# Softmax sums from a column of ones, keys laid by group, and two pieces of expert work moved into step 11 of a fused window-attention and expert kernel

## The chip, the cores and the metric

The kernel runs on one core of one Trainium2 chip. The metric is the device time of one execution in microseconds (us). Before the change three runs took 647.63, 648.9 and 649.51 us, a median of 648.9. One further execution was profiled: it took 648.28 us, of which 646.4 us are the span from the first to the last instruction. Engines are named as the profile names them: PE is TensorE (matmuls; PEld its weight loads), DVE is VectorE, ACT is ScalarE, POOL is GpSimd, and SP is the engine whose queue issues most of the DMAs.

## What is computed

Two layers follow one another: causal attention in a window of 64 positions, and a layer of eight experts of which each token uses one.

```python
# q, k, v: (8, 8, 576, 64) float32: batch, heads, positions, head size
scores = q @ k^T / 8                       # only 0 <= pos_q - pos_k < 64 counts, the rest is masked
attn   = exp(scores - max) / (sum + 1e-9)
x      = (attn @ v), heads side by side    # 4608 tokens x 512
logits = x @ w_gate + modality_bias[modality_id]       # 4608 x 8
e      = argmax(logits);  gate = softmax(logits)[e]
out    = gate * (relu(x @ w1[e]) @ w2[e])              # w1 512 x 1024, w2 1024 x 512, float32
```

## The kernel before

**Tiling.** The 4608 tokens are 72 blocks of 64 positions, and two blocks are a *pair* (36 pairs of 128 rows). A window of 64 means that a block needs its own keys and those of the block before it. Two pairs are a *group* (4 blocks); queries and keys are loaded and turned (transposed on PE) by group.

**Steps.** The attention is written as a loop over `s` (40 steps), software pipelined by hand: step `s` makes the scores of pair `s` (`scores`, PE), masks them and takes each row's minimum of the negated scores (`minima`, DVE, eight heads, L577), takes the exponentials (`exps`, ACT, eight heads, L589, each with a row sum by `accum_out`), turns the exponentials of pair `s-1` (`probs_t`, PE, copied out by ACT at L598), multiplies those of pair `s-2` with the values (`values`, PE, L615), divides by the sum (`values_out`, DVE: a reciprocal at L621 and one product of 128x512 at L623), turns the result (`x_t`) and makes the gate's logits of pair `s-3`. In each step two *heads* pieces of the next group follow: in even steps the keys, `K0` (heads 0 to 3) and `K1` (heads 4 to 7), in odd steps the queries, `Q0` and `Q1`. Each is four transposes on PE and one copy of 128x512 out of PSUM (`heads_out`, L539); K1 is copied by ACT, the other three by DVE. Between these parts `tick(n)` emits up to n small operations on DVE from a list: the routing of tokens, and tables of a few words that choose experts and rows.

The order is fixed by the program (a manual schedule): every engine runs its list in that order, and semaphores order the engines against each other. [...]

**Values.** `vo` holds a pair's own values. `ve` holds for the first of the two blocks the rows in the order in which its window stands: its lower half is copied by POOL from the pair's own rows, its upper half by DVE from the pair before (`swap_v`, L495).

**Expert work.** From step `FIRST` = 12 on, four *pieces* of expert work are put into the gaps of each step (`gap`, `slot_pieces`). A slot is 256 tokens of one expert: `x_part` 0 and 1 turn its rows (L254) and split them into a high and a low part on ACT and DVE (L192, L193), eight `first` pieces multiply by w1 (L279, 12 matmuls of 128x256), eight `second` pieces by w2 (L301, 6 matmuls of 128x512). The rows of a slot come from scratch memory by a DMA that `fetch` issues (L203), behind the indirect DMAs by which POOL scattered them there (L716). The weights of two experts are loaded and split piece by piece from step 3 on (`weights`, L111 on ACT and L116 on DVE). When the attention is over, the remaining pieces follow one another alone.

**PSUM banks.** There are eight: two `tp`, two for scores, one `av`, and `em`, `y0`, `y1` that belong to the expert work. `turn_bank(s)` lends the last three to the attention as long as `s < FIRST - 1`, so up to step 10.

**Start.** Group 0 is turned in two halves by `first_pair(0)` and `first_pair(1)`, one before the scores of step 0 and one between them and the minima. ACT's queue first issues four query DMAs and then the DMAs of the modality numbers, the bias and the gate weights.

## Time and profile before

| | profiled execution |
|---|---|
| its time / its span | 648.28 us / 646.4 us |
| PE busy | 620.0 us (96% of the span) |
| PEld busy | 554.6 us (86%) |
| DVE busy | 367.7 us (57%) |
| ACT busy | 299.4 us (46%) |
| POOL busy | 137.4 us (21%) |
| DMA | 88.07 MB, mean 136 GB/s |
| HBM read, written | 67.49 MB, 23.91 MB |

The page gives shares of the whole span, and the program has stages. From 100 us on, PE is busy for 19.25 to 20.00 us of each stretch of 20 up to 640 us; from 20 to 100 us it is busy for 16.5 to 17.5 of each 20. In the timeline of PE the scores of step 0 start at 9.45 us, those of step 1 at 15.37, of step 2 at 22.25, of step 5 at 40.41, of step 11 at 76.43, of step 12 at 84.85 and of step 13 at 97.65 us. A row of the timeline has start, duration, engine, line, operation, what is written and read, the count, and in brackets the idle time of the engine before it with what ended it. A row of windows has for one stretch the busy time of every engine, the granted clock of PE, and the DMA's share and rate.

### The profile page before, as it was taken

What the parts mean: (1) busy time and instruction counts of PE and PEld (TensorE: products, weight loads), DVE (VectorE), ACT (ScalarE), POOL (GpSimd) and SP (SyncE); (2) the same over time, 40 slices, a digit from 0 to 9 for tenths busy, and PEclk for the clock granted to TensorE, in tenths of its full rate; (3) what the DMA queues carried; (4) which work ended last, traced back from release to release, by engine and by line L of the source; (5) the groups of instructions that cost most, each with busy time, mean ns of one, the idle gap of its engine ahead of it and who ended that gap; (6) DMA issues with size and microseconds to landing.
All of it is one profiled execution on the core that took longest, in us unless ns stands there. A gap on an engine that the chain in (4) does not pass through costs nothing.

```text
span 646.4 us, 17286 instructions
## 1 busy us (share of the span) xinstructions
PE 620.0 (96%) x6508; PEld 554.6 (86%) x6509; DVE 367.7 (57%) x1494; ACT 299.4 (46%) x932; POOL 137.4 (21%) x314
## 2 busy tenths in 40 slices
PE   6888889999999999999999999999999999999996
PEld 4677779898989888889998898899898999989986
DVE  2889967777767686766655365122214524757611
ACT  2789875756565646555544111111113513555411
POOL 4315330232142212320322220011011101101102
PEclk9999989999999999999999999999999999999999
DMA  9988975764876754553412124421041732677300
GB/s 164 195 186 216 212 197 132 196 161 120 181 171 153 159 144 103 144 133 82 132 51 83 50 99 171 157 67 66 23 173 45 236 113 85 218 247 227 120 1 36
DMA packets 138885, 88.07 MB, mean 136 GB/s; under 512 B 116746, under 2 KB 116784, under 8 KB 138672
## 3 DMA queue, kind: packets, MB, share of 16 engines
q1 hardware_dynamic: 130112, 67.44, 42.2%
q0 software_dynamic: 5856, 18.92, 7.8%
q10 hardware_dynamic: 2832, 0.59, 0.6%
q8 instruction: 52, 0.85, 0.6%
q14 instruction: 33, 0.27, 0.2%
HBM read 67.49 MB, written 23.91 MB: 141 GB/s over the span
## 4 chain that ended last, share of the span: by engine, by line
PE 50%; DVE 0%; ACT 0%; issue 0%; POOL 0%; POOLq 0%; ACTq 0%
PE y L301 22%; PE em L279 12%; PE sp L279 10%; PE tp L439 1%; PE y L352 1%; PE av L615 1%; PE em L254 1%; PE tp L254 1%; PE sp L327 0%; PE em L327 0%; PE tp L640 0%; PE sp L563 0%; DVE xa L623 0%; ACT ss L589 0%; DVE hl L288 0%
## 5 line engine op out<-in xcount | busy, mean ns | idle before, releaser
L301 PE MATMUL y<-Whi,hh 128*128 128x512 f32 x288 | 118.7, 412 | 0.0
L301 PE MATMUL y<-Wlo,hh 128*128 128x512 f32 x288 | 112.9, 392 | 0.0
L301 PE MATMUL y<-Whi,hl 128*128 128x512 f32 x288 | 112.8, 392 | 0.0
L589 ACT ACTIVATE ss<-ss,mn 128x128 f32<-128x128 f32 x288 | 112.5, 397 | 0.0
L279 PE MATMUL em<-xh,Whi 128*128 128x256 f32 x400 | 103.5, 293 | 1.2 <-ACT xh L192 0.7
L279 PE MATMUL em<-xh,Wlo 128*128 128x256 f32 x400 | 98.5, 280 | 0.0
L288 DVE SCALAR_TENSOR_TENSOR hl<-em,hh 128x512 fp32r<-128x512 f32 x50 | 34.5, 690 | 92.9 <-ACT hh L287 91.3
L312 POOL DMA_INDIRECT out_dram<-y,id x36 | 37.3, 1036 | 224.6 <-DVE y L309 145.9
L279 PEld LDWEIGHTS em<-xh,Whi 128*128 128x128 f32 x400 | 75.9, 190 | 2.6 <-ACT xh L192 0.9
L279 PEld LDWEIGHTS em<-xh,Wlo 128*128 128x128 f32 x400 | 75.8, 190 | 0.9
L287 ACT ACTIVATE hh<-em 128x512 fp32r<-128x512 f32 x50 | 29.6, 592 | 93.3 <-PE em L279 89.4
L577 DVE CUSTOM_DVE_ANT_0 ss<-sp,masks 128x128 f32<-128x128 f32 x288 | 63.5, 286 | 13.4 <-PE sp L563 13.4
L598 ACT COPY pT<-tp 128x512 f32<-128x512 f32 x58 | 32.2, 589 | 78.0 <-PE tp L439 78.0
L301 PEld LDWEIGHTS y<-Whi,hl 128*128 128x128 f32 x288 | 54.1, 188 | 12.3
L279 PE MATMUL em<-xl,Whi 128*128 128x256 f32 x400 | 63.4, 281 | 0.0
L301 PEld LDWEIGHTS y<-Whi,hh 128*128 128x128 f32 x288 | 54.1, 188 | 7.5
L301 PEld LDWEIGHTS y<-Wlo,hh 128*128 128x128 f32 x288 | 54.3, 188 | 7.1
L589 ACT ACTIVATION_READ_ACCUMULATOR ss<-ss,mn 128x1 f32 x288 | 55.8, 194 | 0.0
L716 POOL DMA_INDIRECT xs_scratch<-xa,idx x36 | 36.3, 1007 | 89.1 <-DVE lm L659 26.9
L279 PEld LDWEIGHTS em<-xl,Whi 128*128 128x128 f32 x400 | 54.2, 189 | 0.0
L288 DVE SCALAR_TENSOR_TENSOR hl<-sp,hh 128x512 fp32r<-128x512 f32 x22 | 15.2, 692 | 61.1 <-ACT hh L287 61.1
L615 PEld LDWEIGHTS av<-ve,pT 128*64 128x64 f32 x576 | 36.4, 138 | 15.2 <-issue 7.4
(242 smaller groups left out, 1243.6 us busy)
## 6 DMA issues: line engine op xcount, KB each, us to landing
xt<-xs_scratch SPq DMA_DIRECT2D x18, 514.0 KB, 4.0
vo<-in_v_dram SPq DMA_DIRECT2D x32, 256.0 KB, 4.1
y<-in_moe_w_dram SPq DMA_DIRECT2D x32, 256.0 KB, 4.0
vo<-in_moe_w_dram SPq DMA_DIRECT2D x24, 256.0 KB, 3.5
ss<-in_moe_w_dram SPq DMA_DIRECT2D x24, 256.0 KB, 3.8
qk<-in_k_dram SPq DMA_DIRECT2D x18, 256.0 KB, 5.5
qk<-in_q_dram SPq DMA_DIRECT2D x18, 256.0 KB, 4.9
xs_scratch<-xs_scratch SPq DMA_DIRECT2D x8, 514.0 KB, 6.0
```

The lines of the kernel that those rows point to most:

```text
L254: nc.tensor.transpose(out=tp[:, n * P:(n + 1) * P].bitcast(F32R), in_=xt[:, t, c * P:(c + 1) * P].bitcast(F32R), identity=ident_r)
L279: nc.tensor.matmul(out=hb[:, i * TP:(i + 1) * TP], lhsT=w[buf][:, c0:c0 + P], rhs=x[:, c * TP:(c + 1) * TP], start=(n == 0), stop=(n == le ...
L287: nc.scalar.activation(out=hh, in_=hb, func=AF.Relu),
L288: nc.vector.scalar_tensor_tensor(out=hl, in0=hb, scalar=0.0, in1=hh.bitcast(F32), op0=ALU.max, op1=ALU.subtract)))
L301: nc.tensor.matmul(out=sl["y", t], lhsT=h[:, i * TP + t * P:i * TP + (t + 1) * P], rhs=w[buf][:, c0:c0 + DM], start=(k == 0 and n == 0), s ...
L312: ins = nc.gpsimd.indirect_dma_start(out=out, out_offset=bass.IndirectOffsetOnAxis(ap=sl["id"][:, t:t + 1], axis=0), in_=y, in_offset=None ...
L352: nc.tensor.matmul(out=yp[:, cols], lhsT=sl["h", n][lo][:, c * P:(c + 1) * P], rhs=w[buf][:, c0 + cols.start:c0 + cols.stop], start=(m == ...
L577: nc.vector.tensor_tensor_reduce(out=ss[a][:, hp, :], in0=sp[a][:, hp * P:(hp + 1) * P], in1=mask, scale=-1.0 / 8.0, scalar=3.0e38, op0=AL ...
L589: nc.scalar.activation(out=ss[a][:, hp, :], in_=ss[a][:, hp, :], func=AF.Exp, bias=mn[:, h:h + 1], scale=-1.0, accum_out=sm[:, h:h + 1])
L598: nc.scalar.copy(out=pT, in_=pp)
L615: nc.tensor.matmul(out=av[c * W64:(c + 1) * W64, 2 * hp + a], lhsT=pT[:, i:i + W64], rhs=(vo if c else ve)[p][:, 2 * hp + a, :], start=Tru ...
L716: ins = nc.gpsimd.indirect_dma_start(out=xs, out_offset=bass.IndirectOffsetOnAxis(ap=idx[:, j:j + 1], axis=0), in_=xg[j], in_offset=None)
```

## The change

What is done differently, by the parts of the title line of the change:

1. **Sums from a column of ones** (pairs 0 to 11). The value tiles `vo` and `ve` become fixed tiles with 65 columns per head, of which the last holds 1.0. The product of exponentials and values has 65 columns, and its last is the row sum. `exps` has no `accum_out` for these pairs, and the addition of 1e-9 moves from POOL (`sums`) to two operations of 128x4 on DVE in `values_out`. Eight heads of 65 columns do not fit one bank, so the product goes to `av` and `y1`, and the division is two products of 128x256 in place of one of 128x512.
2. **Keys by group.** `kT` and `qT` are laid out by half of the ring first and by head pair second (`place`), so that the four blocks of a group lie together for all heads that one copy writes. In the waits of the built program the scores of odd steps had waited on ACT ahead of their last four of sixteen matmuls; in the change they wait on DVE alone.
3. **Heads in arrival order.** The first half of group 0 is turned in the order in which its four DMAs are issued (even rows of keys, of queries, odd rows of keys, of queries), each copy is cut in two, one half for DVE and one for ACT. The second half is turned after the exponentials of heads 0 to 4 in step 0 are emitted and no longer before the minima. The three small DMAs on ACT's queue come after the first half, `select_bias` goes from step 0 to step 1.
4. **Empty rows in step 4**: the DMA that writes two blocks of empty rows goes from step 2 to step 4.
5. **Four banks to step 11**: `turn_bank` lends `em` and `y0` up to step 11, and `y1` to nobody.
6. **Heads of 7 groups ahead**: groups 1 to 7 (before: 1 to 4) are loaded a step earlier, into four places of the later weight buffer.
7. **The slot's rows in step 11**: the first slot is fetched at the start of step 11, with more ticks in step 10, and its two `x_part` pieces are emitted at the end of step 11. Every later piece stands two places earlier. The next slot's fetch is three pieces later for the first four slots.
8. Beside these: the copy of Q1 goes from DVE to ACT for steps under 12, and the upper half of `ve` is copied at the start of a step under 12 (`swap_upper`), not after its minima.

```diff
@@ slot_pieces
-                    if k == 2 and i == 1:
+                    if (k, i) == ((3, 0) if slots_done < 4 else (2, 1)):
                         nxt = fetch()
@@ tiles
-    kT = att.tile([P, HP, RING, W64], F32, name="kT")
-    qT = att.tile([P, HP, RING, W64], F32, name="qT")
+    kT = att.tile([P, 2 * HP * GBLK, W64], F32, name="kT")
+    qT = att.tile([P, 2 * HP * GBLK, W64], F32, name="qT")
+    def place(g, hp):
+        a, j = divmod(g, GBLK)
+        return (a * HP + hp) * GBLK + j
+    vos = [att.tile([P, H, D + 1], F32, name=f"vo{i}") for i in range(3)]
+    ves = [att.tile([P, H, D + 1], F32, name=f"ve{i}") for i in range(2)]
-    AHEAD = 1, 2, 3, 4
+    AHEAD = range(1, 8)
@@ turn_bank
-        if s < FIRST - 1 and i % 5 > 1:
-            return ps_m.tile([P, 512], F32, name=("em", "y0", "y1")[i % 5 - 2])
+        if s < FIRST and i % 4 > 1:
+            return ps_m.tile([P, 512], F32, name=("em", "y0")[i % 4 - 2])
@@ exps
-                bias=mn[:, h:h + 1], scale=-1.0, accum_out=sm[:, h:h + 1])
+                bias=mn[:, h:h + 1], scale=-1.0, accum_out=sm[:, h:h + 1] if p >= FIRST else None)
@@ values_out
+        if p < FIRST:
+            for i in range(2):
+                nc.vector.tensor_scalar(
+                    out=rs[:, i * HP:(i + 1) * HP], in0=av[i][:, :, D], scalar1=1e-9, scalar2=None, op0=ALU.add)
         nc.vector.reciprocal(out=rs, in_=rs)
-        nc.vector.tensor_tensor(
-            out=xa[:, 0:DM].rearrange("p (h d) -> p h d", d=D), in0=st.pop((p, "av")),
-            in1=rs[:, :, None].broadcast_to([P, H, D]), op=ALU.mult)
+        parts = [(av[i][:, :, 0:D], i * HP, HP) for i in range(2)] if p < FIRST else [(st.pop((p, "whole")), 0, H)]
+        for part, h0, n in parts:
+            nc.vector.tensor_tensor(...)
@@ start
+    both = nc.vector.tensor_copy, nc.scalar.copy
+    def first_pair(i, copies):
+        tps = [turn_bank(0) for _ in "kq"]
+        for t in range(2):
+            for nm, tp in zip("kq", tps):
+                first_heads_t(nm, i, t, tp)
+        for nm, tp, c in zip("kq", tps, copies):
+            first_heads_out(nm, i, tp, c)
-    first_pair(0)
+    first_pair(0, (both, both))
+    nc.scalar.dma_start(out=mod_i, ...)    # and brow, wg: from ahead of the first pair
@@ step loop
-        n_tick = 6 if s < FIRST else 5
+        if s == FIRST - 1:
+            fetched.append(fetch())
+        n_tick = 9 if s == FIRST - 2 else 6 if s < FIRST else 5
+        if 1 <= s < FIRST:
+            swap_upper(s - 1)
             if s == 0:
                 keep_warm(WARM[1])
-                first_pair(1)
             minima(s)
@@
-        if s == FIRST - 1:
-            fetched.append(fetch())
         if s < NPR:
             exps(s, (2, 3, 4))
+        if s == 0:
+            first_pair(1, (both[:1], both[1:]))
@@
-            heads_out(tp, G, *heads[1], nc.scalar.copy if heads[1] == K1 else nc.vector.tensor_copy)
+            heads_out(tp, G, *heads[1], nc.scalar.copy if heads[1] == K1 or s < FIRST else nc.vector.tensor_copy)
@@
+        if s == FIRST - 1:
+            for _ in range(2):
+                gap(it)
         if s == 0:
+            choose()
+        if s == 1:
             select_bias()
-            choose()
-        if s == 2:
+        if s == 4:
             nc.sync.dma_start(out=xs_blk[DUMMY:DUMMY + 2].rearrange("b p c -> p b c"), in_=padrow)
```

Three places show how instructions move. The first is DVE, from the split of a weight piece at the end of step 5 to the first minimum of step 6 (`rs` is the reciprocal's tile, `xa` the attention's result, `lg` the logits). Before:

```order
L116 TENSOR_TENSOR Wlo_66<-y,Whi_65 128x512
L621 RECIPROCAL rs<-rs 128x8
L623 TENSOR_TENSOR xa_105<-av,rs 128x512
L645 TENSOR_TENSOR lg<-tp,bias_sel 128x8
L577 ISA ss,mn<-sp_999,masks 128x128
```

and in the change:

```order
L116 TENSOR_TENSOR Wlo_66<-y,Whi_65 128x512
L515 COPY ve_111<-vo_108 64x520
L657 TENSOR_SCALAR rs<-av 128x4
L657 TENSOR_SCALAR rs<-y_980 128x4
L659 RECIPROCAL rs<-rs 128x8
L662 TENSOR_TENSOR xa_105<-av,rs 128x256
L662 TENSOR_TENSOR xa_105<-y_980,rs 128x256
L684 TENSOR_TENSOR lg<-y_1002,bias_sel 128x8
L599 ISA ss,mn<-sp_1017,masks 128x128
```

The copy of `ve` has come ahead of the division from behind the minima; two additions are new, and the one product has become two halves.

The second place is ACT at the start of the program. Before:

```order
L817 ACTIVATE warm<-warm 1x1
L820 DMA y<-in_moe_modality_id_dram 36x256
L822 DMA brow<-in_moe_modality_bias_dram 128x16
L825 DMA wg<-in_moe_w_gate_dram 128x4x8
L551 COPY qT<-tp 128x4x2x64
L551 COPY qT<-y_288 128x4x2x64
L589 ACTIVATE ss,sm<-ss,mn 128x128 x8
L539 COPY kT<-tp 128x2x2x128
```

and in the change:

```order
L856 ACTIVATE warm<-warm 1x1
L566 COPY kT<-tp 128x2x2x64
L566 COPY qT<-tp 128x2x2x64
L977 DMA y<-in_moe_modality_id_dram 36x256
L978 DMA brow<-in_moe_modality_bias_dram 128x16
L980 DMA wg<-in_moe_w_gate_dram 128x4x8
L611 ACTIVATE ss<-ss,mn 128x128 x5
L566 COPY qT<-y_308 128x4x2x64
L611 ACTIVATE ss<-ss,mn 128x128 x3
L550 COPY kT<-tp 128x2x2x128
```

The halves of the first copies stand ahead of the small DMAs, and the second half of group 0 stands behind five exponentials.

The third place is PE where the first slot's rows `xt` are turned. Before, this is in step 12, with the attention's own transposes (`ss` exponentials, `xa` results, `qk` heads) between:

```order
L439 MATMUL tp<-ident_r,ss 128x128 x8
L254 MATMUL em<-ident_r,xt 128x128 x4
L439 MATMUL tp<-ident_r,xa_101 128x128 x4
L254 MATMUL tp<-ident_r,xt 128x128 x4
L439 MATMUL tp<-ident_r,qk 128x128 x4
L279 MATMUL em<-xh,Whi_65 128x256
```

and in the change it closes step 11, with the product of exponentials and values of step 12 behind it:

```order
L441 MATMUL tp<-ident_r,ss 128x128 x8
L441 MATMUL em<-ident_r,xa_105 128x128 x4
L441 MATMUL y_1761<-ident_r,Whi_64 128x128 x4
L722 LDWEIGHTS tri
L722 MATMUL tp<-oh,tri 128x16
L726 LDWEIGHTS ones
L726 MATMUL tp<-oh,ones 128x16
L726 LDWEIGHTS ones
L726 MATMUL tp<-oh,ones 128x8
L441 MATMUL tp<-ident_r,Whi_64 128x128 x4
L254 MATMUL em<-ident_r,xt 128x128 x4
L254 MATMUL tp<-ident_r,xt 128x128 x4
```

The first matmul of the slot's `first` piece follows in step 12 in the gap in which the first `x_part` stood before.

More of the change, by code (lines that the diff above doesn't have):

```diff
@@ L373, in slot_pieces @@
         NK = NC2 // 2
+        slots_done = 0
         sl = fetch()
@@ L563, in scores @@
                 nc.tensor.matmul(
-                    out=sp[a][c * W64:(c + 1) * W64, hp * P:(hp + 1) * P], lhsT=qT[rows, hp, g + c, :],
-                    rhs=kT[rows, hp, win[c], :], start=True, stop=True)
+                    out=sp[a][c * W64:(c + 1) * W64, hp * P:(hp + 1) * P], lhsT=qT[rows, place(g + c, hp), :],
+                    rhs=kT[rows, win(c, hp), :], start=True, stop=True)
         st[p, "sp"] = sp
@@ L695, in route3 @@
         xg = [st.pop((GB * G + j, "xa")) for j in range(GB)]
-        tgt = small.tile(sh3, F32, name="tgt")
+        tgt = small.tile(sh3, F32, name="wn")
         nc.vector.tensor_tensor(
@@ L860, in tile_window_attn_moe @@
                     pattern=[[1, W64]], channel_multiplier=-1)
+    for t in vos + ves:
+        nc.gpsimd.memset(t[:, :, D:], 1.0)
+    nc.gpsimd.memset(ves[0][W64:P], 0.0)
     nc.gpsimd.memset(first_oh, 0.0)
```

102 lines of the change are left out of this document (62 added, 40 removed).

## The prediction

> **What bounds the kernel now.** I read four views: busy time in stretches of 20 us, the same by step, the timelines of PE, DVE and ACT where the steps turn, and the groups of the page. The stretches:
>
> ```profile
> 60.00:80.00 20.00, 16.52 (x312) 14.29 (x311) 19.05 (x105) 17.58 (x66) 8.65 (x16) 1.00 0.99 229
> 100.00:120.00 20.00, 20.00 (x269) 17.92 (x268) 15.38 (x69) 13.74 (x48) 3.62 (x7) 1.00 0.44 117
> 620.00:640.00 20.00, 20.00 (x125) 17.68 (x125) 4.75 (x7) 3.45 (x6) 2.44 (x5) 1.00 0.06 24
> ```
>
> Columns: length, then busy time of PE, PEld, DVE, ACT, POOL, granted clock, DMA share, GB/s. From 100 us to the end PE is full. The amount of expert work is the same before and after, so whatever lets PE's unbroken work begin earlier, or puts pieces of it into earlier idle time, moves the end by that much, and nothing else does unless it opens a new gap. Before 100 us PE has gaps and DVE is the full engine. By steps (8 and 9 together, then 12 and 13):
>
> ```profile
> 58.62:70.19 11.57, 10.29 (x208) 9.14 (x205) 11.11 (x60) 10.90 (x45) 4.48 (x8) 1.00 0.97 222
> 84.85:97.65 12.80, 10.85 (x136) 9.70 (x132) 8.24 (x34) 8.00 (x26) 5.18 (x10) 0.87 0.98 256
> 97.65:108.31 10.66, 10.66 (x145) 9.62 (x141) 7.94 (x36) 6.78 (x23) 0.90 (x3) 1.00 0.34 88
> ```
>
> In the timeline DVE has no idle stretch in steps 8 and 9; ACT at 10.90 of 11.57 is close behind. Step 13, with four pieces and PE full, takes 10.66 us; step 12 with the same work 12.80. I follow one milestone through, the first minimum of a step on DVE, and then the scores of step 13.
>
> **A. The start.** Timelines of DVE and PE:
>
> ```profile
> 7.88 0.69 DVE L551 COPY kT<-tp 128x512 f32<-128x512 f32 x1 [6.65 <-PE tp L439]
> 9.45 1.99 PE L563 MATMUL sp<-kT,qT 64*64 64x128 f32 x32 [0.75 <-ACT qT L551]
> 12.89 0.76 PE L439 MATMUL em<-ident_r,qk 64*128 64x64 f32 x8
> 13.69 0.69 DVE L551 COPY kT<-em 128x512 f32<-128x512 f32 x1 [5.12 <-PE em L439]
> 14.30 0.28 DVE L577 CUSTOM_DVE_ANT_0 ss<-sp,masks 128x128 f32<-128x128 f32 x1
> 15.37 0.40 PE L563 MATMUL sp<-kT,qT 64*64 64x128 f32 x2
> 18.97 0.29 DVE L577 CUSTOM_DVE_ANT_0 ss<-sp,masks 128x128 f32<-128x128 f32 x1 [2.20 <-PE sp L563]
> ```
>
> The scores of step 0 end at 11.4, but their minima wait until 14.30, since DVE's order has the second half of the keys first, and that waits 5.12 us. In the change the minima follow the scores directly. The first copies run as two halves on both engines; halves of one bank go one after the other in the built order, so of the 1.6 us from 7.88 to 9.45 I count 0.9 as saved by the interleaving of K and Q halves, and none by halving as such. Scores of step 0 then start near 8.5 and their minima near 10.4. The transposes of the second half start at about 12.0 (12.89 less 0.9); from there to the scores of step 1 PE now needs 2.5 (12.89 to 15.37), so these start near 14.5. Their operands are there by then: the second half's copies end 0.8 + 0.6 after its transposes start (13.69 and 14.30 against 12.89). With 1.2 for the scores themselves, the first minimum of step 1 comes near 15.7 in place of 18.97: **-3.3 us**. Bounds: -2.5, if the copies save nothing (0.8 less), to -3.8, if the halves really run side by side.
>
> The Trainium skill ("PSUM — Partial Sum Buffer", section "PSUM bank collisions raise a hardware error") says that two engines must not be in one bank and quarter of the partitions at the same time, and that software must keep them apart. The built order agrees (the second half waits for the first); no run shows the case itself. Without it the sum would have the -3.8 here.
>
> **B. Keys by group.** The scores of odd steps stop ahead of their last eight matmuls for ACT's copy of K1, and DVE waits behind them:
>
> ```profile
> 36.53 0.29 DVE L577 CUSTOM_DVE_ANT_0 ss<-sp,masks 128x128 f32<-128x128 f32 x1 [0.57 <-PE sp L563]
> 42.27 0.45 PE L563 MATMUL sp<-kT,qT 64*64 64x128 f32 x8 [0.97 <-ACT kT L539]
> 42.88 0.29 DVE L577 CUSTOM_DVE_ANT_0 ss<-sp,masks 128x128 f32<-128x128 f32 x1 [1.25 <-PE sp L563]
> ```
>
> The odd step's own pair lies in the group that was already complete, so in the new layout the wait is for nothing real and is gone. DVE's two waits add to **-1.8 us** (0.57 + 1.25). Bounds: 0, if in these steps a DMA or ACT turns out just behind, to -1.8; steps 6 to 10 show no such idle time, so there is nothing more.
>
> **C. DVE's work, steps 2 to 11.** Rows of one step:
>
> ```profile
> 58.53 0.17 DVE L704 TENSOR_SCALAR se<-se 128x2 f32<-128x2 f32 x1
> 58.62 0.17 DVE L706 TENSOR_REDUCE dst<-tgt 128x2 f32<-128x16 f32 x1
> 59.54 0.20 DVE L621 RECIPROCAL rs<-rs 128x8 f32<-128x8 f32 x1
> 59.82 0.69 DVE L623 TENSOR_TENSOR xa<-av,rs 128x512 f32<-128x512 f32 x1
> 60.43 0.15 DVE L645 TENSOR_TENSOR lg<-y,bias_sel 128x8 f32<-128x8 f32 x1
> 62.30 0.42 DVE L502 COPY ve<-vo 64x512 f32<-64x512 f32 x1
> 69.43 0.68 DVE L539 COPY qT<-tp 128x512 f32<-128x512 f32 x1
> 70.03 0.16 DVE L702 TENSOR_REDUCE se<-ex 128x2 f32<-128x16 f32 x1
> ```
>
> What an instruction costs is the distance to the next start. A small TENSOR_SCALAR costs 0.09 when nothing depends on it at once (58.53 to 58.62), and about 0.2 to 0.28 when the next needs its result (59.54 to 59.82). Two of them ahead of the reciprocal: 0.08 + 0.20. No row shows a strided 128x4 read out of PSUM; the nearest is L645, of 128x8 out of PSUM, at 0.07 to 0.15. The product of 0.61 in two halves costs one more fixed part, 0.07. So **+0.35 a step**, +3.5 over ten steps; between +0.2 (both pipelined) and +0.7 (each at the full 0.28 and the halves at 0.14 more). The Q1 copy leaves DVE: 0.60 in each of five odd steps, **-3.0**. It lands on ACT, which loses per step eight reads of accumulators:
>
> ```profile
> 74.52 0.40 ACT L589 ACTIVATE ss<-ss,mn 128x128 f32<-128x128 f32 x1
> 74.81 0.20 ACT L589 ACTIVATION_READ_ACCUMULATOR ss<-ss,mn 128x1 f32 x1
> 74.90 0.40 ACT L589 ACTIVATE ss<-ss,mn 128x128 f32<-128x128 f32 x1
> ```
>
> Two exponentials start 0.38 apart, and of this at least 0.09 is the read (74.81 to 74.90). Eight times 0.09 is 0.7 a step or 1.4 in two steps, against 0.6 for the copy, so ACT is lighter and its copy costs nothing; without that cover it would be 0.6 in every second step, 3.0 us. The copies of 64x520 in place of 64x512 and one small copy moved into step 1 add some 0.3 (8/512 of 0.42 in ten steps, and one small row of 0.2). PE's 65th columns are 16 in 1024 and lie in PE's gaps. Sum of C: **+0.8**, bounds -0.7 to +4.3.
>
> **D. Steps 11 to 13.** DVE's first minimum of step 11, and what follows:
>
> ```profile
> 79.27 0.28 DVE L577 CUSTOM_DVE_ANT_0 ss<-sp,masks 128x128 f32<-128x128 f32 x1
> 81.52 0.15 DVE L151 TENSOR_TENSOR e_at<-e_first,e_take 1x1 f32<-1x1 f32 x1
> 82.03 0.67 DVE L539 COPY qT<-tp 128x512 f32<-128x512 f32 x1
> 83.46 0.69 DVE L539 COPY qT<-tp 128x512 f32<-128x512 f32 x1 [0.67 <-PE tp L439]
> 84.85 1.10 PE L563 MATMUL sp<-kT,qT 64*64 64x128 f32 x32
> 86.84 0.54 PE L254 MATMUL em<-ident_r,xt 128*128 128x128 f32 x4
> 90.22 0.39 PE L279 MATMUL em<-xh,Whi 128*128 128x256 f32 x1 [0.56 <-DVE xl L193]
> 91.64 0.58 PE L279 MATMUL em<-xh,Whi 128*128 128x256 f32 x1 [0.68 <-ACT xh L192]
> ```
>
> The minimum moves by A + B + C = -4.3, and two things go ahead of it that stood behind: the copy of `ve` (0.42) and four table operations (0.51, 81.52 to 82.03), to 75.9. Behind it those 0.93 are missing, and the second query copy with its wait (0.67 + 0.60) is on ACT and in another bank: of the 5.58 us from minimum to the scores of step 12 some 4.1 stay, with the slot's eight transposes (1.0, beside DVE's copies). Scores of step 12 near 80.0, before 84.85. Both splits of the rows are then on hand, so the waits of 0.56 and 0.68 go, and step 12 runs as step 13 does now: 10.66. Scores of step 13 near **90.6, before 97.65: 7.0 earlier**. And by then four `first` pieces are done where there were two. One takes PE 1.5 us (165.77 to 167.25, below): **3.0 more**. Gain 10.0. It includes the clock: 0.87 over 12.80 us is 1.7 us lost in step 12, which I let vanish, since PE's work there gets denser.
>
> The Trainium skill ("TensorE: Matmul & The Clock Gate", section "What's actually happening") puts the half clock down to an idle window of about 3.4 us. The trace differs: right ahead of 91.64 PE's idle times were 0.56 and 0.68, and yet step 12's clock is 0.87. By the page a dense step would not dip; if the dip comes from short gaps as here, a rest may stay, and the sum would be up to 1.7 worse.
>
> **E. The later fetch.** Rows of a slot take their time to land, and the piece that needs them comes two pieces sooner:
>
> ```profile
> xt<-xs_scratch SPq DMA_DIRECT2D x18, 514.0 KB, 4.0
> 165.57 0.63 POOL L263 COPY gate<-xt 128x2 f32<-128x2 f32 x1 [4.71 <-DMA xt<-xs_scratch]
> 165.77 0.36 PE L279 MATMUL em<-xh,Whi 128*128 128x256 f32 x1
> 167.25 0.60 PE L439 MATMUL tp<-ident_r,qk 128*128 128x128 f32 x4
> 169.63 0.54 PE L254 MATMUL em<-ident_r,xt 128*128 128x128 f32 x4
> ```
>
> Here the rows land just before 165.57, and `x_part` stands at 169.63. Two gaps earlier is 165.77: 0.2 us of slack. The first three slots have about 1.1, 0.2 and 0.7. I take **+0.4** for one of them late, bounds 0 to 1.5 (one late by half a landing of 4.0, less slack). The fetch of the first slot at the start of step 11 is issued when its table is ready, near 73.5, lands near 77.5, and PE asks for it at about 77.5: nothing, with 0.5 to either side in the range. The pad rows in step 4, the earlier loads of groups 5 to 7 and the small DMAs move no wait that shows on DVE; the DMA share near 1.0 is the objection (below).
>
> **Sum.** The profiled execution took 648.28. 648.28 - 10.0 + 0.4 = 638.7; the median of the runs shown lies 0.6 above the profiled one, so **639.3 us**.
>
> **The rivals.** 0.3%, 1.9 us, is about what a measurement of this kernel can tell from no change.
> 1. *Half of it.* DVE's additions at the upper price (+3.5), or step 12 keeps a wait for `xl` and the dip (+2.9). For it: DVE's 11.11 of 11.57, so each added operation is paid in full. Against: the rows above are short. 641.5 to 646. Chance 0.20.
> 2. *Transfers pace the steps.* For it: a share of 0.97 to 0.99 in steps 8 to 12. Against: DVE has no idle time there, and rates go to 256 GB/s where the work asks. If true, A and B (5.1) are lost and D's second half stays: 643 to 646.5. Chance 0.06.
> 3. *No change.* The slot's fetch or its transposes hold up the scores of step 12 behind them on PE, so that step 12 begins where it began: only the pieces remain, and the late rows take them back: 647 to 650.8. Chance 0.06.
> 4. *Slower.* The fetch three pieces later makes each of four slots late. A piece is 2.66 us (10.66 / 4); distance from fetch to need shrinks by three pieces, 8 us. If scatter and fetch do not already wait for each other, each `x_part` waits some 3 us and PE, which runs in order, with it: 12 us, against the 10.0 won: 651. It decides as soon as the four waits exceed 3.0 us each (10.0 and the 1.9 of the bound, by four). Against: in the trace the landing, not the issue, is already set by the scatter. Chance 0.06.
>
> My forecast, 636.5 to 641.5, has 0.62. The range 636 to 646 holds it and the rivals of the same sign, about 0.82. Faster 0.87, the same 0.07, slower 0.06.
>
> **What would show it.** First minimum of step 1 near 15.7; no wait of DVE for scores in steps 5 to 7; a pair of steps still 11 to 11.7 us with DVE full; scores of step 12 near 80, of step 13 near 90.6, clock 1.00 there; PE without gaps for `xt` at the ends of the first four slots. It is wrong if the small additions cost over 0.3 us each, if PE waits at `x_part`, or if DMA becomes what DVE waits for in steps 2 to 10.

## The result, and the profile after

| | before | changed |
|---|---|---|
| median | 648.73 us (647.63 to 649.51, 4 runs) | 657.61 us (654.97 to 659.95, 4 runs) |
| ratio | | 1.0137, 95% interval 1.0099 to 1.0175 |
| profiled execution's span | 646.4 us | 658.1 us |

The change is slower by 8.9 us; 639.3 had been forecast. The profiled run of the changed kernel took 659.95 us, the longest of the four; its mean granted clock is 0.989, that of the other three 0.987, 0.989 and 0.996. Its windows, with the columns that the prediction explained: first the steps 11, 12 and 13, then a stretch of steps 11 and 12, then all from 20 us to step 11.

```profile
71.41:83.53 12.12, 7.66 (x115) 6.83 (x112) 9.74 (x54) 7.62 (x19) 3.45 (x7) 0.74 0.94 268
83.53:99.58 16.05, 14.19 (x151) 13.48 (x149) 7.25 (x33) 7.67 (x25) 1.15 (x3) 0.77 0.35 85
99.58:110.25 10.67, 10.67 (x145) 9.71 (x141) 7.94 (x37) 6.91 (x23) 0.80 (x3) 1.00 0.32 80
...
79.70:87.10 7.40, 7.40 (x97) 6.93 (x97) 4.08 (x21) 2.06 (x5) 3.56 (x7) 0.50 0.45 144
...
20.00:71.00 51.00, 45.66 (x884) 39.97 (x884) 47.80 (x286) 41.91 (x116) 17.04 (x27) 1.00 1.04 223
```

The windows begin where the scores of a step begin: those of step 11 at 71.41 us (76.43 before), of step 12 at 83.53 (84.85), of step 13 at 99.58 (97.65). So 5.0 us were won by step 11, and steps 11 and 12, some 18.5 us by the sum of the prediction (72.1 to 90.6), took 28.2 (21.2 before). In the 7.4 us from 79.7 on PE is busy throughout, at half the clock.

Step 13 begins 1.9 us late, yet the span is 11.7 longer: the rest is lost later. The list of what PE waited for (sum in us, times, longest), changed kernel:

```profile
PE em L254 <- DMA xt<-xs_scratch: 6.5, 4, 2.9
PE tp L722 <- DVE qT L550: 6.0, 5, 1.7
PE em L441 <- DVE xa L662: 2.2, 1, 2.2
...
PE em L279 <- DVE wn L703: 1.9, 1, 1.9
```

The largest entries of this list before were values for DVE (3.6) and the first loads (3.3), and neither slot rows nor the routing matmuls stood in it. The first two entries belong to part 7: `x_part` waits for the slot's rows (2.2 us in step 11, 3.1 from step 13 to step 35, 1.2 later), and the routing matmuls of L722 wait for DVE's copy of Q0, five times. From the scores of step 13 to those of step 35 it takes 247.7 us (347.28 - 99.58), before 237.05: 10.65 us more, all in steps 15, 19, 23, 27, 31 and their neighbours. One of these places, DVE and ACT in step 19:

```profile
173.25 0.69 DVE L193 TENSOR_TENSOR xl<-em,xh 128x512 fp32r<-128x512 f32 x1 [2.56 <-ACT xh L192]
173.86 0.68 DVE L550 COPY qT<-tp 128x512 f32<-128x512 f32 x1
```

```profile
172.13 0.60 ACT L111 CAST Whi<-y 128x512 fp32r<-128x512 f32 x1
172.64 0.57 ACT L192 CAST xh<-em 128x512 fp32r<-128x512 f32 x1
```

```profile
174.59 0.17 PE L722 MATMUL tp<-oh,tri 128*128 128x16 bf16 x1 [1.70 <-DVE qT L550]
```

Two pieces earlier, `x_part` falls into the middle of an odd step. Its split waits on DVE for ACT's high part, which stands behind three exponentials and a weight cast; DVE's next instruction is the copy of Q0, which would have been ready, and PE needs the bank that this copy empties. The same chain stands in steps 15, 23, 27 and 31.

### The profile page after: what moved, and what is told of

It reads as the page before. It is cut to its first block, busy times and chain, and to the rows that moved or that the text cites. A ratio compares the mean times of both kernels' runs of the same rounds, so it can differ in the third digit from the quotient of the medians.

```text
span 658.1 us, 17179 instructions
## 1 busy us (share of the span) xinstructions
PE 623.4 (95%) x6508; PEld 558.8 (85%) x6509; DVE 367.0 (56%) x1525; ACT 294.2 (45%) x843; POOL 134.6 (20%) x307
## 5 line engine op out<-in xcount | busy, mean ns | idle before, releaser
L611 ACT ACTIVATE ss<-ss,mn 128x128 f32<-128x128 f32 x288 | 106.2, 397 | 5.6 <-DVE mn L599 5.6
L279 PEld LDWEIGHTS em<-xh,Wlo 128*128 128x128 f32 x400 | 75.9, 190 | 1.0
L287 ACT ACTIVATE hh<-sp 128x512 fp32r<-128x512 f32 x22 | 13.2, 598 | 76.5 <-PE sp L279 76.5
L585 PE MATMUL sp<-kT,qT 64*64 64x128 f32 x1152 | 42.7, 284 | 2.0 <-ACT qT L550 1.3
```

Of the source, the lines that this page charges most:

```text
L279: nc.tensor.matmul(out=hb[:, i * TP:(i + 1) * TP], lhsT=w[buf][:, c0:c0 + P], rhs=x[:, c * TP:(c + 1) * TP], start=(n == 0), stop=(n == le ...
L287: nc.scalar.activation(out=hh, in_=hb, func=AF.Relu),
L585: nc.tensor.matmul(out=sp[a][c * W64:(c + 1) * W64, hp * P:(hp + 1) * P], lhsT=qT[rows, place(g + c, hp), :], rhs=kT[rows, win(c, hp), :], ...
L611: nc.scalar.activation(out=ss[a][:, hp, :], in_=ss[a][:, hp, :], func=AF.Exp, bias=mn[:, h:h + 1], scale=-1.0, accum_out=sm[:, h:h + 1] if ...
```

## The experiments

Medians in us. "Without 7" is the change with its part 7 undone. Before measured 648.39 to 648.73 beside them.

| kernel | median (lowest to highest) | ratio, 95% interval |
|---|---|---|
| change without 7 | 641.77 (640.76 to 642.95) | 0.9891 (0.9865 to 0.9918) |
| before with 7 alone | 661.16 (660.74 to 661.78) | 1.0190 (1.0167 to 1.0213) |
| change, warm matmuls in step 11 | 654.33 (652.64 to 656.06) | 1.0086 (1.0054 to 1.0118) |
| change, Q0 ahead of the gap | 649.88 (644.87 to 654.45) | 1.0012 (0.9985 to 1.0038) |
| change, rows in 11, later pieces back | 644.84 (642.22 to 649.83) | 0.9939 (0.9907 to 0.9972) |
| the same, fetch first, warm matmuls | 643.84 (642.32 to 645.58) | 0.9921 (0.9897 to 0.9945) |
| without 7, fetch early only | 641.13 (640.53 to 643.63) | 0.9893 (0.9862 to 0.9924) |
| without 7, Q1 on DVE | 644.50 (643.38 to 645.99) | 0.9929 (0.9902 to 0.9957) |
| without 7, sums by accum_out | 647.09 (643.86 to 648.95) | 0.9962 (0.9936 to 0.9988) |
| without 7, old layout | 647.47 (646.12 to 650.10) | 0.9982 (0.9960 to 1.0003) |
| without 7, old start | 644.52 (643.54 to 645.33) | 0.9940 (0.9916 to 0.9963) |
| without 7, warm start | 642.66 (642.00 to 643.44) | 0.9903 (0.9879 to 0.9927) |
| without 7, old layout, Q1 on DVE | 644.76 (643.68 to 646.12) | 0.9936 (0.9910 to 0.9962) |
| without 7, accum_out, Q1 on DVE | 643.87 (640.69 to 645.26) | 0.9896 (0.9861 to 0.9931) |
| change with three repairs | 651.60 (649.81 to 652.71) | 1.0041 (1.0026 to 1.0056) |

### Part 7 undone, and part 7 alone

```diff
-                    if (k, i) == ((3, 0) if slots_done < 4 else (2, 1)):
+                    if k == 2 and i == 1:
-        if s == FIRST - 1:          # start of the step
-            fetched.append(fetch())
-        n_tick = 9 if s == FIRST - 2 else 6 if s < FIRST else 5
+        n_tick = 6 if s < FIRST else 5
+        if s == FIRST - 1:          # behind x_t, as before the change
+            fetched.append(fetch())
-        if s == FIRST - 1:          # end of the step
-            for _ in range(2):
-                gap(it)
```

> The change without its part 7: the first slot is fetched in the middle of step 11 again, its two x_part pieces stand in step 12, every later piece stands where it stood before, and the next slot is fetched at the old place. Theory 1 (part 7 alone turned a gain into a loss): the scores of step 11 stay near 71.4 us as in the change (76.4 before), step 12 has again some 12.8 us, no waits of PE of over 1 us after 100 us; total 641 to 644.5 us. Theory 2 (the other parts hurt the later steps as well, by the banks, the loads ahead or the order of the small operations): the waits of PE for the routing and for rows after 120 us remain, total 650 us or more.

Measured 641.77: theory 1. Scores of step 11 at 71.54, of step 13 at 91.30, then 236.9 us to step 35, with no wait of PE for rows or for the routing in its list after step 12. The reverse edit puts the same lines into the kernel before:

> The kernel before with part 7 alone. Theory 1: the late rows, the half clock and the waits in every fourth step are there without any of the other parts: 648.7 + 8.9 + 5 = 660 to 664 us. Theory 2 (part 7 hurts only because the other parts make steps 2 to 11 shorter, so that scatter and fetch come too late for it): here step 11 begins 5 us later, the rows are in time, total 645 to 651 us.

Measured 661.16: theory 1 again. 12.8 us are lost without any other part (from 648.39), and PE's list shows the same entries as the change:

```profile
PE tp L685 <- DVE qT L541: 6.0, 5, 1.7
...
PE em L254 <- DMA xt<-xs_scratch: 2.7, 4, 1.4
...
PE em L279 <- DVE wn L666: 1.9, 1, 1.9
```

(L685 is the routing there, L541 the copy of Q0.) So the other seven parts together make the kernel 6.6 us faster, and part 7 costs 15.8 on top of them (641.77 to 657.61).

### Which pieces of part 7 cost what

The first edit puts warm matmuls on zeros where PE idles in step 11:

```diff
         if s == FIRST - 1:
+            keep_warm(8)
             for _ in range(2):
                 gap(it)
```

> The change with eight matmuls of 128x512 on zeros put on PE at the end of step 11, ahead of x_part, where PE waits 2.2 us for the slot's rows. Theory 1 (PE's idle time in step 11 pulls the granted clock down in 80 to 100 us, 0.73 there, and this costs some 5 us of PE's time): the clock stays over 0.9 there, step 12 falls from 16.05 to 12 to 13 us, total 652 to 654.5 us. Theory 2 (the clock falls anyway, or step 12 is set by waits): the clock stays near 0.73 or step 12 stays near 16, total 656 to 659 us.

Measured 654.33, 3.3 us less: theory 1. Step 12 (from 83.23 us) and the stretch from 80 us:

```profile
83.23:95.83 12.60, 10.74 (x153) 10.19 (x149) 7.76 (x37) 7.68 (x25) 2.66 (x7) 1.00 0.59 146
80.00:100.00 20.00, 17.80 (x259) 16.15 (x258) 13.71 (x65) 12.18 (x38) 4.96 (x9) 1.00 0.52 138
```

The clock is 1.00, where the change had 0.77 in this step, and step 12 takes 12.60 in place of 16.05; it holds the same wait of 1.9 for `em`. So the half clock is a cost of the change. That the wait for rows brings it is not shown: by the means of the windows the change's clock falls at 77.29 us and that wait begins at 77.45. The wait ahead of it, 2.24 us for `xa`, stands in the change without part 7 too (1.57), where the clock stays at 1.00. In the two later kernels with the same warm matmuls (rows in 11 with the early fetch, and the three repairs) the clock falls in the same place, at 76.92 and 78.34, but is back after 3.4 us. In the kernels without them (the change, Q0 ahead of the gap, rows in 11) it stays at half for 10.2, 13.7 and 13.7 us. What goes with the warm matmuls in these traces is an early return of the clock. The Trainium skill ("TensorE: Matmul & The Clock Gate", section "What's actually happening") asks for an idle window of about 3.4 us for the half clock. The trace differs: in the 3.4 us ahead of 77.29 PE was busy for 1.5 us, with transposes and small routing matmuls.

The second edit moves the first transposes and copy of a step ahead of the gap in steps 15, 19, 23, 27, 31:

```diff
+        early = heads and s > FIRST and s % 4 == 3
+        if early:
+            (Q0's transposes and copy)
         if n_gap > 0:
             ...
             gap(it, True)
-        if heads:
+        if heads and not early:
```

> The change with the transposes and the copy of Q0 ahead of the second gap in steps 15, 19, 23, 27, 31 (the steps in which x_part now stands), so that DVE copies Q0 before it waits for the high part of the slot's rows. Theory 1 (in these steps PE waits 1.2 to 1.7 us ahead of the routing matmuls because its bank is freed by the Q0 copy, which queues on DVE behind a split that waits for ACT): these five waits vanish, total 5 to 7 us less than the change, 650.5 to 653 us. Theory 2 (the rows themselves come late, and the wait only moves to the first piece that needs them): total 656 to 659 us, and PE waits ahead of L279 or L254 instead.

Measured 649.88, 7.7 us less and a little under theory 1's range. The runs lie 9.6 us apart, and the clock goes with them: the longest, 654.45, which is the profiled one, has a mean clock of 0.987, the shortest, 644.87, one of 0.998. The five routing waits are gone from the trace and steps 13 to 35 last 239.3 us in place of 247.7. Waits for rows stay:

```profile
PE em L254 <- DMA xt<-xs_scratch: 4.8, 3, 2.8
```

Of these 2.8 us are in step 11 and 1.2 after step 35; from step 13 to step 35 0.8 are left of 3.1, so not all of the 8.4 us is the routing's. Theory 1, then, with the lateness of rows as a second, smaller cost. The next kernel keeps the rows in step 11, but does only two pieces in step 12, so that all later ones stand as before:

```diff
-                    if (k, i) == ((3, 0) if slots_done < 4 else (2, 1)):
+                    if k == 2 and i == 1:
-        n_gap = 0 if s < FIRST else 4
+        n_gap = 0 if s < FIRST else 2 if s == FIRST else 4
```

> The change with the first slot's fetch and x_part in step 11 as it has them, but with only two pieces in step 12 in place of four, so that every piece from step 13 on stands where it stood before, and the next slot is fetched at the old place. It parts the two halves of part 7. Theory 1 (steps 11 and 12 lose by late rows and half clock, the later steps lose only because x_part falls into the odd step): steps 13 to 35 last 237 us as without part 7 (248 in the change), no waits ahead of the routing; step 11 still 12 us, step 12 some 11, total 643.5 to 647 us. Theory 2 (the loss of the later steps comes from the rows of the first slot, by a delay that is carried on): total 652 us or more.

Measured 644.84: theory 1. Steps 13 to 35 last 238.0 us (335.68 - 97.69), no routing waits. Its step 11 still waits 3.3 us for rows. The profiled execution is the longest of the eight (649.83 us, clock 0.988); the shortest took 642.22 us at 0.998. The next kernel adds the eight warm matmuls to this one, and issues the fetch ahead of step 11's query loads:

```diff
+        if s == FIRST - 1:
+            fetched.append(fetch())
         for f, args in at.pop(s, ()):
             f(*args)
-        if s == FIRST - 1:
-            fetched.append(fetch())
...
+            keep_warm(8)
```

> The kernel of the run before this one in the list, with the first slot's fetch ahead of step 11's query loads on SP and eight warm matmuls ahead of x_part. Theory 1: the rows land 1 us earlier or so, the clock stays at 1.00 in step 12, step 11 takes 10 to 11 us and step 12 some 9; total 639.5 to 642.5 us, level with the change without part 7 or better. Theory 2 (the scatter, not SP's order, sets the landing): the rows land at 79.5 us again, and only the clock is mended, 642 to 644 us.

Measured 643.84, in theory 2's range and, with overlapping intervals, not to be told from the run before it. The two SP timelines, first the change's, then this kernel's:

```profile
71.18 3.39 SPq L536 DMA_DIRECT2D Whi<-in_q_dram  x2
75.60 0.39 SPq L203 DMA_DIRECT2D xt<-xs_scratch  x1
```

```profile
70.07 0.85 SPq L100 DMA_DIRECT2D y<-in_moe_w_dram  x1
74.16 0.39 SPq L203 DMA_DIRECT2D xt<-xs_scratch  x1
```

The fetch goes out 1.4 us sooner, but not before 74.16, when the scatter of the rows, which goes out at 67.86 and lands 5.7 us later, has landed. In the change that scatter went out at 68.25, 0.4 us later, so SP's order cost some 1.0 us of the 1.4. Steps 11 to 13 take 31.4 us together, without part 7 30.4: in these traces rows turned in step 11 win nothing even when PE does not stand idle for them. Fetching early and turning them in step 12 was tried too:

```diff
-                    if (k, i) == ((3, 0) if slots_done < 4 else (2, 1)):
+                    if k == 2 and i == 1:
-        if s == FIRST - 1:          # end of the step; the fetch at its start stays
-            for _ in range(2):
-                gap(it)
```

> The change with the first slot fetched at the start of step 11, tables ahead of it, but with x_part in step 12 and all pieces and fetches where they stood before. Theory 1 (the waits of 0.6 us ahead of the slot's rows and of 0.6 and 0.7 ahead of the first pieces in step 12 come from late rows): steps 11 and 12 together 18.5 to 19.3 us in place of 19.8, total 640.5 to 641.5 us. Theory 2 (the tables ahead of the minima of step 11 cost DVE 0.5 us, and the waits come from ACT and DVE in step 12): no gain, 641.5 to 643 us.

Measured 641.13: steps 11 and 12 take 19.55 in place of 19.76, the wait of 0.64 ahead of `x_part` is gone, the waits ahead of the first pieces (0.56, 0.68) are not. The total lies in theory 1's range, the two steps between the theories, and the total is not to be told from 641.77. This and the change without part 7 are the fastest kernels found, 1.1% under the kernel before.

Three of these edits on the whole change at once (Q0 ahead of the gap, fetch ahead of the loads, eight warm matmuls, each as shown above):

> The whole change, part 7 included, with three repairs at once: Q0 ahead of the second gap in every fourth step, the first slot's fetch ahead of step 11's loads, and eight warm matmuls ahead of x_part. Theory 1 (the mechanisms are separate and add: 7.7 for Q0, 3.3 for the clock, 1 for the fetch, against 657.6): 644.5 to 647.5 us, no routing waits, clock over 0.95 in 80 to 100 us, the wait of 1.9 in step 12 left. Theory 2 (they overlap): 648 to 651 us.

Measured 651.60, 6.0 less than the change and not the 12 of the single sums; theory 2's range ends at 651. In the profiles each repair does act where it was put: steps 11 and 12 take 24.4 us (28.2 in the change), steps 13 to 35 take 242.1 (247.7). But 2.8 of what the Q0 repair alone had won after step 13 are lost again, above all in steps 24, 28 and 32, which take 11.44 to 11.87 in place of 10.88. In each of these three PE stops once among the logits' matmuls (0.45, 0.46 and 0.30 us), and the profile shows nothing that it waited for. Why is open.

### What the other parts are worth

```diff
-            heads_out(..., nc.scalar.copy if heads[1] == K1 or s < FIRST else nc.vector.tensor_copy)
+            heads_out(..., nc.scalar.copy if heads[1] == K1 else nc.vector.tensor_copy)
```

> The change without part 7, and with the copy of Q1 on DVE again (part 8's first half undone). Theory 1 (DVE sets steps 2 to 10, so 0.60 in each of five odd steps comes back in full): 644 to 645.5 us, against 641.8; a pair of steps 11.9 to 12.0 us in place of 11.36. Theory 2 (ACT's queue is what sets the pairs, since undoing the sums made them longer): 641 to 642.5 us or less, pairs unchanged.

Measured 644.50, 2.7 more: theory 1 by the total, at the size of term C (3.0), though steps 7 and 8 took 11.63 us and not 11.9 to 12.0. Then part 1 undone, `accum_out` and POOL's addition for all pairs:

```diff
-                bias=..., scale=-1.0, accum_out=sm[:, h:h + 1] if p >= FIRST else None)
+                bias=..., scale=-1.0, accum_out=sm[:, h:h + 1])
-        if p < FIRST:              # in values and values_out: column, second bank, halves
+        if p < 0:
```

> The change without part 7, and with the row sums by accum_out on ACT and the addition on POOL again for all pairs (part 1 undone; the value tiles keep their 65 columns). It asks what part 1 is worth. Theory 1 (DVE alone sets steps 2 to 10, so that its two additions and the split product cost 0.3 a step): total 638 to 639.5 us, against 641.8 with the column. Theory 2 (with the copy of Q1 on ACT, ACT at 10.9 of 11.57 us a pair of steps would be full with the eight reads of accumulators a step, 1.4 a pair): a pair of steps is 11.6 to 12 us in place of 11.36, total 642.5 to 645 us.

Measured 647.09, 5.3 more: theory 1 is out, and the loss is above theory 2's range. Windows of steps 7 and 8, first of the change without part 7, then of this kernel, and one row of this kernel's DVE:

```profile
48.76:60.15 11.39, 10.40 (x207) 9.08 (x203) 10.38 (x63) 10.29 (x30) 3.65 (x6) 1.00 1.02 226
```

```profile
53.61:65.02 11.41, 10.16 (x207) 9.18 (x204) 10.01 (x58) 10.20 (x38) 4.27 (x8) 1.00 0.96 221
```

```profile
48.55 0.29 DVE L599 CUSTOM_DVE_ANT_0 ss<-sp,masks 128x128 f32<-128x128 f32 x1 [1.88 <-PE sp L585]
```

These two steps are nearly alike. The difference lies in others: ahead of step 6's minima DVE waits 1.88 us for scores, nothing there with the column, and step 6 takes 8.07 us in place of 5.64; steps 8 to 10 take 18.7 in place of 17.1. Behind DVE's wait stands PE, and behind PE stands ACT's copy of Q1, as PE's row in step 6 shows:

```profile
47.51 0.67 PE L585 MATMUL sp<-kT,qT 64*64 64x128 f32 x16 [1.30 <-ACT qT L550]
```

That copy starts at 46.86, directly behind the last exponential with its read, and ACT has no idle stretch in the 3.5 us before. From 20 to 80 us PE's scores wait 6.3 us for this copy, with the column 2.1. So ACT, with eight reads a step and the copy, sets these steps. The half clock has a share too: in step 6 it lasts for 3.4 us. Then part 2 undone, the old order of keys and queries:

```diff
     def place(g, hp):
-        a, j = divmod(g, GBLK)
-        return (a * HP + hp) * GBLK + j
+        return hp * 2 * GBLK + g
```

> The change without part 7, and with keys and queries laid by head pair first again (part 2 undone). Theory 1 (the waits of the odd steps' scores for ACT's copy of K1 come back, 0.6 to 1.3 us each in steps 5 and 7, on DVE's path): total 643 to 644.5 us, waits of DVE for scores in the first odd steps. Theory 2 (ACT, rid of the accumulator reads, copies K1 in time, so the layout is worth nothing beside part 1): 641 to 642.5 us.

Measured 647.47, 5.7 more: more than theory 1 gave. PE's list has waits on ACT for keys and for queries:

```profile
PE sp L584 <- ACT kT L549: 3.4, 4, 1.1
PE sp L584 <- ACT qT L549: 2.2, 4, 0.8
```

The second of these stands in the list of the change without part 7 as well (2.1, 5, 0.8); the old layout brings the first. Were these worths their own, or owed to the copy of Q1 on ACT? Each was undone together with it, by the two edits above.

> The change without part 7, with the old layout of keys and queries and with the copy of Q1 on DVE. Theory 1 (with Q1 on DVE the old layout costs only the waits of the odd steps, 1.8 us, so that the rest of the 5.7 that it cost alone was the scores waiting on ACT's copy of Q1): 645.5 to 647 us, that is 1 to 2.5 above the run with Q1 on DVE (644.5), and not above the run with the old layout alone (647.5). Theory 2 (the layout is worth 5 us whatever copies Q1): 649 to 651 us.

> The change without part 7, with the row sums by accum_out and with the copy of Q1 on DVE. Theory 1 (the column's worth is the room on ACT for Q1; without that copy ACT is not full, and DVE is 0.3 a step lighter by the column's absence): 642 to 645 us, below the 647.1 of the sums undone alone. Theory 2 (ACT sets the steps with the eight reads in any case): 646.5 to 649 us.

Measured 644.76 and 643.87, against 644.50 with Q1 on DVE alone. Theory 2 is out for both; the first lies even under its theory 1's range, the second in it. With Q1 on DVE neither the layout nor the column can be told from nothing by these medians. All three together give 641.8, two of them 644.5, 647.1 and 647.5, the column alone 644.8, the layout alone 643.9, so they have to be priced together. How much of each difference is the order itself is another question, taken up below.

The start, with the second half of group 0 ahead of the first minima again:

```diff
                 keep_warm(WARM[1])
+                first_pair(1, (both[:1], both[1:]))
             minima(s)
...
-        if s == 0:
-            first_pair(1, (both[:1], both[1:]))
```

> The change without part 7, and with the second half of group 0 ahead of the first minima again (that half of part 3 undone; the order of arrival and the halves of the copies stay). Theory 1 (DVE's minima of step 0 wait for the second half's keys, as in term A): first minimum of step 1 at 17.5 to 18.3 us in place of 15.8, total 643.5 to 645 us. Theory 2 (the start is set by the loads, and the order is made up for in step 2): 641.5 to 643 us.

Measured 644.52, 2.75 more; DVE's timeline:

```profile
12.87 0.69 DVE L566 COPY kT<-em 128x512 f32<-128x512 f32 x1 [4.44 <-PE em L441]
16.43 0.29 DVE L599 CUSTOM_DVE_ANT_0 ss<-sp,masks 128x128 f32<-128x128 f32 x1 [0.59 <-PE sp L585]
```

DVE stands idle ahead of that half's keys with the minima behind, as before. Step 1's first minimum is at 16.43, less late than theory 1 had it; the total is within its range.

These differences hold more than the order of work. In the profiles (scores of step 11: when they start; step 0 and step 12: how long they last; half clock: how much of step 12 ran at it, all in us):

| without 7, and | step 0 | scores of step 11 | step 12 | half clock |
|---|---|---|---|---|
| nothing else | 5.87 | 71.54 | 12.23 | 0 |
| Q1 on DVE | 7.24 | 75.34 | 12.16 | 0 |
| sums by accum_out | 7.23 | 77.33 | 14.26 | 3.4 |
| old layout | 5.78 | 74.02 | 15.37 | 6.8 |
| old start | 5.97 | 71.86 | 13.45 | 3.4 |
| old layout, Q1 on DVE | 5.67 | 72.89 | 12.29 | 0 |
| accum_out, Q1 on DVE | 7.23 | 73.99 | 13.47 | 3.4 |

So of the old layout's 5.7 us the profile shows 2.5 by step 11 and 3.1 in step 12; all ten of its runs have a mean clock of 0.993 or 0.994, where the four runs of Q1 on DVE and the six of the old layout with Q1 on DVE have 0.998 or 0.999. The old start loses 0.3 us by step 11 and 1.2 in step 12 (its profile is the shortest of its four runs). With accum_out and Q1 on DVE two runs at a clock of 0.998 took 640.69 and 641.10 us, no more than all parts but 7 together. The worths of single parts are therefore open by some 3 us; that part 7 costs 15.8 is not touched by this.

Last, more matmuls ahead of the first rows:

```diff
-    WARM = 4, 3
+    WARM = 8, 3
```

> The change without part 7, and with eight matmuls on zeros in place of four before the first rows land, which fills 1.6 us of PE's idle time from 3.2 us on. Some profiles of the changed kernels have step 0 at 5.7 to 5.9 us and others at 7.2 us, with transposes of 128x128 at twice the duration up to 17 us. Theory 1 (PE's activity before 5 us decides when the full clock is granted): step 0 always 5.4 to 5.9 us, all runs within 1.5 us of each other, median 640 to 641.5 us. Theory 2 (chance, or the first rows are delayed by the extra matmuls): runs spread over 2 us or more as now, median 641 to 643 us.

Measured 642.66, step 0 at 7.23: theory 1 is out and the median is in theory 2's range, though the runs lie only 1.4 us apart, where it had 2 or more. More on this at the end.

## Why the prediction was wrong

**Where the sum went.** The profiled span, 658.1, misses the forecast for it (646.4 less the 9.6 of the sum) by 21.3 us: some 9.0 by the scores of step 13 (99.58 against 90.6), 10.2 from there to step 35, and 2.1 in what follows. The steps that failed are D and E.

**A, the start: right in its number, in part by luck.** First minimum of step 1 forecast at 15.7, measured 15.53. In the run with the order of minima and second half put back it comes at 16.43, and without part 7 at 15.80, so that order gave 0.6 to 0.9 us, where the working had put 2.4 on it; the rest came with the other edits. And the profile has the fast course of the start (see the end): in the seven profiles with the slow one the scores of step 1 start at 15.63 to 16.06, here at 14.37.

**B, the layout, and C, DVE's work: right in sum, wrong in their parts.** The first minimum of step 11 was forecast at 75.9:

```profile
75.95 0.28 DVE L599 CUSTOM_DVE_ANT_0 ss<-sp,masks 128x128 f32<-128x128 f32 x1
```

The division's rows in step 11 of the change:

```profile
74.70 0.16 DVE L657 TENSOR_SCALAR rs<-av 128x4 f32<-128x4 f32 x1
...
75.88 0.16 DVE L684 TENSOR_TENSOR lg<-y,bias_sel 128x8 f32<-128x8 f32 x1
```

They take 1.18 us, before 0.89 (59.54 to 60.43): +0.29 a step where +0.35 was put down. Q1's copy was worth 2.7 where 3.0 was put down. But "ACT is lighter and its copy costs nothing" holds only beside the column: with `accum_out` the scores waited 6.3 us for this copy. And the 1.8 of the layout were put down as if it stood alone: with Q1 on DVE it could not be told from nothing. The parts were costed one by one and depend on one another.

**D, steps 11 to 13: failed, and with it the forecast.** Three steps of its working were wrong.
- "lands near 77.5, and PE asks for it at about 77.5: nothing". The rows landed at 79.54. The working took the table as what sets the issue; SP's two query loads ahead of it (to 74.57) and a scatter that lands at 73.9 were in the queue as well. PE waited 2.23 us, with the products and scores of step 12 behind it.
- "Both splits of the rows are then on hand, so the waits of 0.56 and 0.68 go". A longer one took their place, 1.86 us: all four pieces of step 12 now are `first` pieces and write the bank `em`, and the third waits until ACT and DVE have emptied it of the first two (DVE's `hl` starts at 92.24, PE's piece at 93.08).
- Of the clock's 1.7 us: "which I let vanish, since PE's work there gets denser". The loss before was one stretch at half clock (91.57 to 94.97). The change has one from 77.29 to 87.53, which begins behind the first of its waits in step 11, and one from 94.36 to 97.77; the clock is 0.74 and 0.77 in steps 11 and 12, and the kernel with warm matmuls, whose profile has no half clock there, is 3.3 us faster.

**E, the later fetch: failed.** +0.4 was put down, 10.65 measured from step 13 to 35. The landing of rows was a part (3.1 us of waits in this stretch). The larger part was not looked at: a piece that moves within a step takes its ACT and DVE instructions to another place in those engines' queues. The Q0 copy was behind a split that waits for ACT, and PE behind the copy; with Q0 ahead of the gap the five waits, 6.0 us, are gone, and in all 8.4 of the 10.65.

**Two more pieces done, 3.0.** From step 35 to the end the change has 310.8 us, before 311.7. Two waits of 0.57 and 1.21 us of PE in that stretch took some of it.

**The rivals.** Rival 4 had the sign and the place (four late slots, slower) and was given 0.06; its mechanism, late rows alone, is the smaller part (3.1 of the 10.65). Rival 3 named the rows that hold up the scores of step 12. None named the queue on DVE. The 0.87 for faster rested on D, in which every condition had to hold at once. Rival 2, transfers, is out: scores of step 11 came 5.0 us earlier at a DMA share of 1.04 from 20 us on.

## What to carry to other kernels

When a piece of work is moved to where PE has room, list what its helpers on other engines stand behind and in front of at the new place: in an in-order queue a waiting instruction of the moved piece holds up the next one, which may be what PE needs. Price parts that feed one another as one edit, and ask for each "costs nothing" which other part makes it so. Where several parts are put in together, undo the one that leaves the tuned stretch (here the stage with PE already full) first. And before a difference of a few microseconds is put down to an edit, compare the mean clock of the runs on both sides.

## What was not expected of the hardware

The half clock comes in whole pieces of one length. Worked out from the clock of windows 0.5 to 1.1 us long, it lasts in the change from 77.29 to 87.53 and from 94.36 to 97.77, which is 10.24 and 3.41 us with 6.83 between: three times, once and twice 3.41. The windows of the 17 profiled kernels, up to 400 us, have 16 such stretches, and each lasts 3.4, 6.8, 10.2 or 13.7 us. In the 3.4 us ahead of each fall PE had been busy for 1.0 to 2.1 us. The length of a wait does not decide it: the wait of 1.86 us in step 12 was followed by 3.4 us at half clock in the change and by none in the kernel with warm matmuls in step 11. One wait of 2.50 us in the kernel that only fetches early was not followed by any; its step 11:

```profile
70.78:78.75 7.97, 5.46 (x107) 4.66 (x103) 7.49 (x48) 5.43 (x16) 0.46 (x2) 1.00 0.99 215
```

And the start has two courses. Two kernels with the same order of work there, the change without part 7 (first row) and that with the rows in step 11 and later pieces back (second row):

```profile
13.62 1.09 PE L441 MATMUL tp<-ident_r,Whi 128*128 128x128 f32 x8
```

```profile
13.79 1.97 PE L441 MATMUL tp<-ident_r,Whi 128*128 128x128 f32 x8
```

Eight transposes take 1.09 or 1.97 us, and step 0 takes 5.7 to 6.0 or 7.2 us. The windows give a clock of 1.00 for both, so that the full clock comes later in the second is read from these durations alone. Of thirteen profiled kernels with this start seven had the slow course. That and the half clock later on are a part of why runs of these kernels lie further apart than those before. Eight matmuls ahead of the first rows in place of four did not help: the first transposes then ran in 0.68 us in place of 1.08, and the clock was half from 7.5 to 17.75 us.
